# Decode attention with FFN on one core: a cut-up load ring that keeps twice as much V, with interleaved parts and warm-up matmuls

## The chip, the cores and the metric

The kernel runs on one core of a Trainium2 chip. The metric is the device time of one execution in microseconds. A verdict of faster or slower needs 2%.

In the profiles PE is TensorE running matmuls, PEld its weight loads, DVE VectorE, ACT ScalarE, POOL GpSimd, and SP the engine that issues the loads. PEclk, the granted clock, is the part of its full clock that TensorE was allowed. The DMA share is the time that the packets took, as a share of the time of 16 DMA engines; it can come out slightly above 1.

## The reference

Eight sequences (B = 8), one new token each, go twice through an attention block and an FFN block. Both attention blocks read the **same** K and V caches.

```python
# x: (8, 1, 640); k_cache, v_cache: (8, 32, 4096, 128); wq: (640, 4096); wo: (4096, 640)
def _A_ref(x, k_cache, v_cache, wq, wo):
    q = heads(x @ wq)                                        # 32 heads of 128
    p = softmax(einsum("bhqd,bhkd->bhqk", q, k_cache) * Dh ** -0.5)
    return flat(einsum("bhqk,bhkd->bhqd", p, v_cache)) @ wo
def _B_ref(x, w1, w2):
    return relu(x @ w1) @ w2                                  # 640 -> 1728 -> 640
x = x + A(layernorm(x)); x = x + B(layernorm(x))
x = x + A(layernorm(x)); x = x + B(layernorm(x))
```

K and V are 256 MiB each in bf16 and are used twice, so without reuse 1 GiB has to come from HBM. Layer 1 of a sequence needs all of its layer 0, so a K or V tile read for layer 0 can serve layer 1 only if it stays in SBUF for that long.

## The kernel before

The unit of work is a *visit*: one pair of heads of one sequence in one layer, 256 visits in all. A K or V tile of a visit is [128 partitions, 64 keys, 128], 2 MiB; each partition receives one contiguous run of 16 KiB. Visits of layer 0 of the next sequence stand between the two layers of a sequence, to give its FFN time.

```python
RING = 4
KEEP = ((0, 64), (1, 32))          # last head pair: 64 of 64 keys of V kept; the one before: 32
...
kv = ctx.enter_context(tc.tile_pool(name="kv", bufs=RING))
...
def load_k(i):
    K_tiles[i] = kv.tile([P, J, Dh], BF16, name="K_sb", tag="kv")
    nc.sync.dma_start(out=K_tiles[i], in_=pair_src(A_k_cache, b, hp))

def load_v(v):                      # (cut)
    if kk and layer == 0:           # stays in SBUF until layer 1
        kept[b, hp] = rpool.tile([P, kk, Dh], BF16, name=f"V_keep{hp}")
        nc.sync.dma_start(out=kept[b, hp], in_=src[:, :kk, :])
    if kk < J:
        V = kv.tile([P, J, Dh], BF16, name="V_sb", tag="kv")
        nc.sync.dma_start(out=V[:, kk:, :], in_=src[:, kk:, :])

def score(i):                       # q.k: multiply on DVE in place, sum over d on PE
    for w in PARTS:                 # 4 parts of 32 of the 128 d
        nc.vector.tensor_tensor(out=part, in0=part, in1=<q broadcast>, op=ALU.mult)
        for k in range(lo, lo + w, RW):
            nc.tensor.matmul(s_tiles[i], lhsT=ident, rhs=K[:, :, k : k + RW], ...)
```

In each loop pass the kernel scores visit i and attends visit i - 3, and loads K two visits ahead and V two visits ahead of its use.

Of the kernel before, what the change touches and what calls it, by code (L numbers as in the profile page):

```python
# [14 lines left out]
RING = 4  # L15
KEEP = ((0, 64), (1, 32))
PARTS = (32, 32, 32, 32)
# [13 lines left out]
def kernel(  # L31
# [12 lines left out]
    nc = tc.nc  # L44
# [22 lines left out]
    kv = ctx.enter_context(tc.tile_pool(name="kv", bufs=RING))  # L67
    rpool = ctx.enter_context(tc.tile_pool(name="rpool", bufs=1))
# [67 lines left out]
    def ln_steps(b0, nb, xln):  # L136
# [26 lines left out]
        def std():  # L163
            st["std"] = sm.tile([P, nb], FP32, name="std", bufs=1)
            nc.scalar.activation(out=st["std"], in_=st["var"], func=ACT.Sqrt, bias=eps_c, scale=1.0 / D)

# [10 lines left out]
    def ffn_steps(layer, b):  # L177
# [3 lines left out]
        cut1 = [f_i * FC // 3 for f_i in range(4)]  # L181
# [21 lines left out]
        def down(k):  # L203
            if k == 0:
                st["y_ps"] = ps.tile([P, DC], FP32, name="ch_ps")
            for c in range(k * DC // 3, (k + 1) * DC // 3):
# [11 lines left out]
        steps += [("P", lambda k=k: up(k)) for k in range(3)] + [("A", relu)]  # L218
        steps += [("P", lambda k=k: down(k)) for k in range(3)] + [("D", add)]
# [7 lines left out]
    FA = 3 * NP // 4  # L227
    FA -= FA % GP
    order0 = list(range(NP))

    NG = NP // GP
    order1 = [hp for g in range(NG - 1, -1, -1) for hp in [NP - NG + g] + list(range(g, NP - NG, NG))]
    order2 = [NP - 1, NP - 3, NP - 2, NP - 4] + order0[:-GP]
    visits = [(0, 0, hp, 1) for hp in order0]
    for b in range(B - 1):
        nxt = [(0, b + 1, hp, 1) for hp in order0]
        if b + 1 < B - 1:
            visits += nxt[:FA] + [(1, b, hp, NG) for hp in order1] + nxt[FA:]
        else:
            cur = [(1, b, hp, 1) for hp in order2]  # L240
            visits += nxt[:FA] + cur[:GP] + nxt[FA:] + cur[GP:]
    visits += [(1, B - 1, hp, NG) for hp in order1]
# [4 lines left out]
    keep = {NP - 1 - n: keys for n, keys in KEEP}  # L247
    last_of = {}
    for v, (layer, b, hp) in enumerate(visits):
        last_of[layer, b] = v  # L250

    K_tiles, V_tiles, kept, qb_tiles, s_tiles, S_tiles, invL_tiles, oT_tiles, oy_tiles, q_tiles = (
        {} for _ in range(10)
    )
    blk_ps = {}

# [3 lines left out]
    def load_k(i):  # L260
        layer, b, hp = visits[i]
        K_tiles[i] = kv.tile([P, J, Dh], BF16, name="K_sb", tag="kv")
        nc.sync.dma_start(out=K_tiles[i], in_=pair_src(A_k_cache, b, hp))

    def load_v(v):

        layer, b, hp = visits[v]
        kk = keep.get(hp, 0)
        src = pair_src(A_v_cache, b, hp)
        pieces = []  # L270
        if kk and layer == 0:
            kept[b, hp] = rpool.tile([P, kk, Dh], BF16, name=f"V_keep{hp}")
            nc.sync.dma_start(out=kept[b, hp], in_=src[:, :kk, :])
        if kk:
            pieces.append((0, kk, kept[b, hp]))
        if kk < J:
            V = kv.tile([P, J, Dh], BF16, name="V_sb", tag="kv")
            nc.sync.dma_start(out=V[:, kk:, :], in_=src[:, kk:, :])
            pieces.append((0, J, V))
        V_tiles[v] = pieces  # L280

    def project_q(i):
# [5 lines left out]
        assert sorted(group) == list(range(first, last, q_step[i]))  # L288
        xl = xlns[layer, b]
# [17 lines left out]
    def score(i):  # L307

        s_tiles[i] = ps.tile([P, J, RW], FP32, name="s_ps", bufs=2)
        K, q = K_tiles.pop(i), qb_tiles.pop(i)  # L310
        lo = 0
        for w in PARTS:
            part = K[:, :, lo : lo + w]
            nc.vector.tensor_tensor(out=part, in0=part, in1=_free(q[:, lo : lo + w], [(0, J), (1, w)]), op=ALU.mult)  # L314
            for k in range(lo, lo + w, RW):
                nc.tensor.matmul(  # L316
                    s_tiles[i], lhsT=ident, rhs=K[:, :, k : k + RW], start=(k == 0), stop=(k + RW == Dh)
                )
# [221 lines left out]
```

## Time and profile before

| | before |
|---|---|
| median time | 2537.75 us (four runs, 2537.68 to 2537.89) |
| moved by DMA | 1065.84 MB |
| PE / DVE busy | 74% / 60% |
| mean granted PE clock | 0.854 |

Slices, queues and chain of waits of the kernel before. In the first three lines each digit or number is one fortieth of the span; DMA digits are busy tenths of the 16 DMA engines, GB/s what they moved.

```profile
PEclk8878898888888889888888888888888888888887
DMA  9999999999999999999999999999999999999997
GB/s 394 415 412 426 427 425 427 426 425 422 423 427 424 427 421 420 427 425 425 427 418 428 425 426 426 417 427 426 426 426 420 426 426 425 410 426 426 427 425 309
DMA packets 83190, 1065.84 MB, mean 420 GB/s; under 512 B 8468, under 2 KB 14292, under 8 KB 17492
q1 hardware_dynamic: 83028, 1063.54, 99.4%
DMA 65%; PE 21%; DVE 14%; issue 0%; ACT 0%; SPq 0%; DVEq 0%; ACTq 0%
...
L314 DVE TENSOR_TENSOR K_sb<-K_sb,qb 128x2048 bf16<-128x2048 bf16 x1024 | 1185.7, 1221 | 422.7 <-DMA K_sb<-in_A_k_cache_dram 422.3
```

The load queue is busy 99.4% of the span, and DVE, which starts each visit, idles 422 us for K. The kernel is bound by DMA.

### The profile page before, as it was taken

The numbers are of one execution on the slowest core, as the hardware profiler recorded it, in microseconds if no ns is written. First come the engines' busy times: TensorE is split into PE (matmuls) and PEld (weight loads), VectorE is DVE, ScalarE is ACT, GpSimd is POOL, SyncE is SP. The second block draws the span as 40 slices with busy tenths as digits, with TensorE's granted clock in tenths as the row PEclk, the third lists the DMA queues.
The fourth block names the chain that finished last, engine by engine and source line by source line (L and its number), as shares of the span: only waits on it lengthen the run. The fifth ranks groups of instructions, "written<-read, shape, count | busy, mean of one in ns | idle before, by whom it ended". The sixth has DMA issues, their size and how long they took to land.

```text
span 2536.4 us, 36119 instructions
## 1 busy us (share of the span) xinstructions
PE 1877.8 (74%) x15270; PEld 870.8 (34%) x15270; DVE 1520.8 (60%) x2476; ACT 504.9 (20%) x1578; POOL 2.1 (0%) x15
## 2 busy tenths in 40 slices
PE   5657777787777877778777787777877777768776
PEld 2223333343333433334333343333433333333333
DVE  5445665666655656656566566656666566656664
ACT  1111211122112222112221122122211122212221
POOL 0000000000000000000000000000000000000000
PEclk8878898888888889888888888888888888888887
DMA  9999999999999999999999999999999999999997
GB/s 394 415 412 426 427 425 427 426 425 422 423 427 424 427 421 420 427 425 425 427 418 428 425 426 426 417 427 426 426 426 420 426 426 425 410 426 426 427 425 309
DMA packets 83190, 1065.84 MB, mean 420 GB/s; under 512 B 8468, under 2 KB 14292, under 8 KB 17492
## 3 DMA queue, kind: packets, MB, share of 16 engines
q1 hardware_dynamic: 83028, 1063.54, 99.4%
q8 instruction: 119, 1.95, 0.3%
q14 instruction: 43, 0.35, 0.0%
HBM read 1063.50 MB, written 0.01 MB: 419 GB/s over the span
## 4 chain that ended last, share of the span: by engine, by line
DMA 65%; PE 21%; DVE 14%; issue 0%; ACT 0%; SPq 0%; DVEq 0%; ACTq 0%
DMA K_sb<-in_A_k_cache_dram 64%; PE s_ps L316 19%; DVE K_sb L314 13%; PE o_ps L379 1%; DMA V_sb<-in_A_v_cache_dram 1%; PE ch_ps L209 0%; PE q_ps L294 0%; ACT o_sb L384 0%; PE blk_ps L361 0%; PE oy_ps L404 0%; PE ch_ps L189 0%; DVE hmx L337 0%; PE oy_ps L390 0%; DVE xT L411 0%; PE blk_ps L333 0%
## 5 line engine op out<-in xcount | busy, mean ns | idle before, releaser
L316 PE MATMUL s_ps<-K_sb,ident 128*128 128x512 bf16 x4096 | 1277.8, 467 | 557.6 <-DVE K_sb L314 524.7
L314 DVE TENSOR_TENSOR K_sb<-K_sb,qb 128x2048 bf16<-128x2048 bf16 x1024 | 1185.7, 1221 | 422.7 <-DMA K_sb<-in_A_k_cache_dram 422.3
L316 PEld LDWEIGHTS <-ident 128*128 128x128 bf16 x4096 | 468.7, 115 | 1267.8 <-issue 794.9
L384 ACT CAST o_sb<-o_ps 104x512 bf16<-104x512 f32 x256 | 150.0, 586 | 1723.0 <-PE blk_ps L333 1195.5
L379 PE MATMUL o_ps<-V_sb,P 128*8 128x512 bf16 x3712 | 250.8, 381 | 4.9 <-DMA V_sb<-in_A_v_cache_dram 4.9
L337 DVE TENSOR_REDUCE hmx<-blk_ps 2x2 f32<-2x128 f32 x128 | 35.6, 278 | 265.9 <-PE blk_ps L333 265.9
L354 ACT ACTIVATE P<-S_sb,nmax 64x64 bf16<-64x64 f32 x512 | 187.1, 365 | 8.5
L326 DVE TENSOR_REDUCE S_sb<-s_ps 128x64 f32<-128x512 f32 x256 | 175.4, 685 | 0.0
L379 PEld LDWEIGHTS <-P 128*8 128x8 bf16 x4096 | 99.2, 85 | 106.7 <-issue 59.3
L411 DVE TENSOR_TENSOR xT<-xT,oy_ps 128x5 f32<-128x5 f32 x256 | 38.6, 151 | 141.0 <-PE oy_ps L404 141.0
L404 PEld LDWEIGHTS <-wo_sb 128*128 128x128 bf16 x2560 | 80.9, 96 | 92.0 <-issue 92.0
L367 DVE RECIPROCAL invL<-blk_ps 128x4 f32<-128x4 f32 x128 | 23.4, 183 | 147.3 <-PE blk_ps L361 147.3
L404 PE MATMUL oy_ps<-oT,wo_sb 128*128 128x1 bf16 x2560 | 103.0, 165 | 0.2 <-DVE oT L397 0.2
L354 ACT ACTIVATION_READ_ACCUMULATOR P<-S_sb,nmax 64x1 f32 x512 | 94.5, 185 | 0.0
L390 PE MATMUL oy_ps<-dsel,o_sb 104*128 104x2 bf16 x1024 | 64.3, 166 | 36.6 <-ACT o_sb L384 36.6
L303 ACT CAST qb<-q_ps 128x512 bf16<-128x512 f32 x64 | 37.5, 586 | 245.7 <-DVE K_sb L314 240.8
L390 PEld LDWEIGHTS <-o_sb 104*128 104x128 bf16 x1024 | 44.5, 98 | 92.6 <-ACT o_sb L384 66.8
L361 PEld LDWEIGHTS blk_ps<-lrow,ones_c 128*128 128x128 f32 x256 | 48.7, 191 | 20.3 <-ACT P L354 1.9
L345 PE MATMUL blk_ps<-diag,onesb_c 2*128 2x4 bf16 x128 | 20.4, 159 | 33.2 <-DVE diag L341 31.5
L209 PE MATMUL ch_ps<-hT,w_sb 128*128 128x1 bf16 x1120 | 43.1, 165 | 2.0 <-ACT hT L200 0.3
L294 PE MATMUL q_ps<-wq_sb,xln 128*64 128x512 bf16 x320 | 41.7, 391 | 2.9 <-DMA wq_sb<-in_A_wq_dram 2.9
L209 PEld LDWEIGHTS <-w_sb 128*128 128x128 bf16 x1120 | 40.1, 96 | 9.4 <-PE oy_ps L404 5.5
(53 smaller groups left out, 503.8 us busy)
## 6 DMA issues: line engine op xcount, KB each, us to landing
K_sb<-in_A_k_cache_dram SPq DMA_DIRECT2D x256, 2048.0 KB, 13.0
V_sb<-in_A_v_cache_dram SPq DMA_DIRECT2D x224, 2048.0 KB, 16.9
V_sb<-in_A_v_cache_dram SPq DMA_DIRECT2D x16, 1024.0 KB, 17.7
V_keep<-in_A_v_cache_dram SPq DMA_DIRECT2D x8, 2048.0 KB, 17.6
V_keep<-in_A_v_cache_dram SPq DMA_DIRECT2D x8, 1024.0 KB
wq_sb<-in_A_wq_dram SPq DMA_DIRECT2D x4, 1280.0 KB, 19.7
wo_sb<-in_A_wo_dram SPq DMA_DIRECT2D x4, 1280.0 KB, 25.7
w_sb<-in_B_w_dram SPq DMA_DIRECT2D x1, 2160.0 KB, 28.6
```

Of the source, the lines that this page charges most:

```text
L209: nc.tensor.matmul(st["y_ps"][:, c : c + 1], lhsT=w2_sb[:fs, f, c * P : (c + 1) * P], rhs=st["hT"][:fs, f : f + 1], start=(f == 0), stop=( ...
L294: nc.tensor.matmul(q_ps[hh * HP : (hh + 1) * HP], lhsT=_free(xl[:, c : c + 1], [(0, HP)]), rhs=wv[:, c, first : last : q_step[i], hh, :], ...
L314: nc.vector.tensor_tensor(out=part, in0=part, in1=_free(q[:, lo : lo + w], [(0, J), (1, w)]), op=ALU.mult)
L316: nc.tensor.matmul(s_tiles[i], lhsT=ident, rhs=K[:, :, k : k + RW], start=(k == 0), stop=(k + RW == Dh))
L326: nc.vector.tensor_reduce(out=S_tiles[k][:, j, :], in_=s_tiles.pop(i), axis=AX.X, op=ALU.add)
L354: nc.scalar.activation(out=P2[k % 2][r, j, :, hh], in_=S[r, j, :], func=ACT.Exp, bias=nmax[r, j, hh : hh + 1], scale=inv_sqrt_dh, accum_ou ...
L361: nc.tensor.matmul(L_ps, lhsT=ones_f, rhs=lrow2[k % 2].rearrange("p j h -> p (j h)"), start=True, stop=True)
L379: nc.tensor.matmul(o_ps[32 * c : 32 * c + 8, :], lhsT=P2[k % 2][:, j, lo : lo + 4, :], rhs=V[:, lo : lo + 4, :], start=(g == 0), stop=(g = ...
L384: nc.scalar.copy(out=o_sb, in_=o_ps[:104, :])
L390: nc.tensor.matmul(oy_tiles[v][:, :2], lhsT=o_sb[:, i, :], rhs=dsel[:104, i, :], start=(i == 0), stop=(i == 3))
L404: nc.tensor.matmul(oy_tiles[v][:, 2 + c : 3 + c], lhsT=wo_sb[:, 2 * hp + hh, c * P : (c + 1) * P], rhs=oT[:, hh : hh + 1], start=(hh == 0) ...
L411: nc.vector.tensor_tensor(out=xT[:, b, :], in0=xT[:, b, :], in1=oy_tiles.pop(v)[:, 2:], op=ALU.add)
```

## The change: its intent, and the diff

Nearly the same SBUF is used otherwise. The ring of four tiles and the separate 1.5 kept tiles become one arena of 11 units of 1 MiB (half the keys of a tile). Loads take two adjacent units where at least four of the five pairs hold no kept half ("whole": 16 KiB per partition), otherwise one unit at a time ("half": 8 KiB per partition). Six halves of V are kept per sequence, 3 tiles for 1.5. Each unit is given back as soon as its half was used. The work of a visit is spread between the four parts of the score; WARM adds two matmuls that compute nothing before each of two of these parts.

```diff
-RING = 4
-KEEP = ((0, 64), (1, 32))
+UNITS = 11
+KEEP = ((0, 2), (1, 2), (2, 1), (3, 1))
+NCUT = 2
+WARM = 2
...
+        nc.scalar.activation(out=st["s1"][:, :1], in_=eps_c, func=ACT.Exp)   # after Sqrt
...
-    FA = 3 * NP // 4
+    FA = NP // 2
...
+    arena = kv.tile([P, UNITS * JH, Dh], BF16, name="arena")
...
+    def roomy():
+        k = kept_units()
+        return sum(1 for u in range(0, UNITS - 1, 2) if not {u, u + 1} & k) >= 4
...
+    def load_whole(which, v):                     # two adjacent units, one DMA
+    def load_half(which, v, h):                   # one unit, half the keys
+    def load_kept(v, h):                          # a half of V that stays for layer 1
...
+    warm_ps = ps.tile([P, 512], FP32, name="warm_ps")
+    def score(i, n):
+        if n % 2 == 0:
+            for _ in range(WARM):
+                nc.tensor.matmul(warm_ps, lhsT=ident, rhs=wq_sb[:, 0, :512], start=True, stop=True)
+        if ("K", i) in pairs:
+            K, j0, nj, lo, w = unit(take("K", i, 0), 2), 0, J, n * Dh // 4, Dh // 4
+        else:                                     # 2 parts of 64 of the d for each half of the keys
+            h = n // 2
+            K, j0, nj, lo, w = unit(take("K", i, h)), h * JH, JH, n % 2 * Dh // 2, Dh // 2
...
+            part(0)
+            ... softmax_sum, gather_o, one FFN piece
+            part(1)
+            ... reduce, max, 1/sum, scale; first half of V if loaded in halves
+            part(2)
+            ... max turned, output projection, one FFN piece
+            part(3)
+            ... rest of V, exp, one FFN piece
```

(Cuts are marked by dots; the order of the visits changes with FA.)

More of the change, by code (lines that the diff above doesn't have):

```diff
@@ L14 @@
 AX = mybir.AxisListType
-RING = 4
-KEEP = ((0, 64), (1, 32))
-PARTS = (32, 32, 32, 32)
+UNITS = 11
+KEEP = ((0, 2), (1, 2), (2, 1), (3, 1))
+NCUT = 2
+WARM = 2
 ENG = mybir.EngineType
@@ L66 @@
     wres = ctx.enter_context(tc.tile_pool(name="wres", bufs=1))
-    kv = ctx.enter_context(tc.tile_pool(name="kv", bufs=RING))
-    rpool = ctx.enter_context(tc.tile_pool(name="rpool", bufs=1))
+    kv = ctx.enter_context(tc.tile_pool(name="kv", bufs=1))
     sm = ctx.enter_context(tc.tile_pool(name="sm", bufs=2))
@@ L180, in ffn_steps @@
         steps = ln_steps(b, 1, xf)
-        cut1 = [f_i * FC // 3 for f_i in range(4)]
+        cut1 = [f_i * FC // NCUT for f_i in range(NCUT + 1)]
         def up(k):
@@ L205, in down @@
                 st["y_ps"] = ps.tile([P, DC], FP32, name="ch_ps")
-            for c in range(k * DC // 3, (k + 1) * DC // 3):
+            for c in range(k * DC // NCUT, (k + 1) * DC // NCUT):
                 for f in range(FC):
@@ L216, in add @@
             nc.vector.tensor_tensor(out=dst[:, b, :], in0=xT[:, b, :], in1=st["y_ps"], op=ALU.add)
-        steps += [("P", lambda k=k: up(k)) for k in range(3)] + [("A", relu)]
-        steps += [("P", lambda k=k: down(k)) for k in range(3)] + [("D", add)]
+        steps += [("P", lambda k=k: up(k)) for k in range(NCUT)] + [("A", relu)]
+        steps += [("P", lambda k=k: down(k)) for k in range(NCUT)] + [("D", add)]
         if layer == 0:
@@ L224, in ffn_steps @@
         return steps
-    FA = 3 * NP // 4
-    FA -= FA % GP
+    FA = NP // 2
     order0 = list(range(NP))
-    NG = NP // GP
-    order1 = [hp for g in range(NG - 1, -1, -1) for hp in [NP - NG + g] + list(range(g, NP - NG, NG))]
-    order2 = [NP - 1, NP - 3, NP - 2, NP - 4] + order0[:-GP]
-    visits = [(0, 0, hp, 1) for hp in order0]
+    top = NP - 2 * GP
+    order1, step1 = [], []
+    if top >= 0:
+        for a in (1, 0):
+            order1 += [NP - 2 + a, top + a, NP - 4 + a, top + 2 + a]
+    step1 = [2] * len(order1) + [1] * (NP - len(order1))
+    order1 += [hp for hp in order0 if hp not in order1]
+    first = [(0, 0, hp, 1) for hp in order0]
+    visits = first
     for b in range(B - 1):
         nxt = [(0, b + 1, hp, 1) for hp in order0]
+        cur = [(1, b, hp, st) for hp, st in zip(order1, step1)]
         if b + 1 < B - 1:
-            visits += nxt[:FA] + [(1, b, hp, NG) for hp in order1] + nxt[FA:]
+            visits = visits + nxt[:FA] + cur + nxt[FA:]
         else:
-            cur = [(1, b, hp, 1) for hp in order2]
-            visits += nxt[:FA] + cur[:GP] + nxt[FA:] + cur[GP:]
-    visits += [(1, B - 1, hp, NG) for hp in order1]
+            visits = visits + nxt[:FA] + cur[:FA] + nxt[FA:] + cur[FA:]
+    visits = visits + [(1, B - 1, hp, st) for hp, st in zip(order1, step1)]
     q_step = [v[3] for v in visits]
@@ L246 @@
     assert NV == 2 * B * NP and NV % 2 == 0
-    keep = {NP - 1 - n: keys for n, keys in KEEP}
+    n_keep = {NP - 1 - n: halves for n, halves in KEEP}
     last_of = {}
@@ L250 @@
         last_of[layer, b] = v
-    K_tiles, V_tiles, kept, qb_tiles, s_tiles, S_tiles, invL_tiles, oT_tiles, oy_tiles, q_tiles = (
-        {} for _ in range(10)
-    )
+    LAG = 3
+    JH = J // 2
+    arena = kv.tile([P, UNITS * JH, Dh], BF16, name="arena")
+    qb_tiles, s_tiles, S_tiles, invL_tiles, oT_tiles, oy_tiles, q_tiles = ({} for _ in range(7))
     blk_ps = {}
+    owner = [None] * UNITS
+    freed = list(range(-UNITS, 0))
+    clock = [0]
+    where = {}
+    pairs = set()
+    kept = {}
@@ L257, in pair_src, with buddy, unit, free @@
+    reserved = set()
+    def buddy(u):
+        return u ^ 1 if u ^ 1 < UNITS else None
+    def unit(u, n=1):
+        return arena[:, u * JH : (u + n) * JH, :]
     def pair_src(cache, b, hp):
         return cache[b, 2 * hp : 2 * hp + 2].rearrange("h (pp j) d -> (h pp) j d", pp=HP)
-    def load_k(i):
-        layer, b, hp = visits[i]
-        K_tiles[i] = kv.tile([P, J, Dh], BF16, name="K_sb", tag="kv")
-        nc.sync.dma_start(out=K_tiles[i], in_=pair_src(A_k_cache, b, hp))
-    def load_v(v):
-        layer, b, hp = visits[v]
-        kk = keep.get(hp, 0)
-        src = pair_src(A_v_cache, b, hp)
-        pieces = []
-        if kk and layer == 0:
-            kept[b, hp] = rpool.tile([P, kk, Dh], BF16, name=f"V_keep{hp}")
-            nc.sync.dma_start(out=kept[b, hp], in_=src[:, :kk, :])
-        if kk:
-            pieces.append((0, kk, kept[b, hp]))
-        if kk < J:
-            V = kv.tile([P, J, Dh], BF16, name="V_sb", tag="kv")
-            nc.sync.dma_start(out=V[:, kk:, :], in_=src[:, kk:, :])
-            pieces.append((0, J, V))
-        V_tiles[v] = pieces
+    def free(u):
+        clock[0] += 1
+        owner[u] = None
+        freed[u] = clock[0]
@@ new lines, in spare, with kept_units, dma @@
+    def spare():
+        us = [u for u in range(UNITS) if owner[u] is None and u not in reserved]
+        return min(us, key=lambda u: freed[u]) if us else None
+    def kept_units():
+        return set(kept.values())
+    def roomy():
+        k = kept_units()
+        return sum(1 for u in range(0, UNITS - 1, 2) if not {u, u + 1} & k) >= 4
+    def dma(u, n, cache, v, h):
+        layer, b, hp = visits[v]
+        nc.sync.dma_start(out=unit(u, n), in_=pair_src(cache, b, hp)[:, h * JH : (h + n) * JH, :])
@@ new lines, in load_whole @@
+    def load_whole(which, v):
+        us = [u for u in range(0, UNITS - 1, 2)
+              if owner[u] is None and owner[u + 1] is None and not {u, u + 1} & (reserved | kept_units())]
+        if not us:
+            return False
+        u = min(us, key=lambda u: max(freed[u], freed[u + 1]))
+        pairs.add((which, v))
+        for h in range(2):
+            owner[u + h] = where[which, v, h] = u + h
+        dma(u, 2, A_k_cache if which == "K" else A_v_cache, v, 0)
+        return True
@@ new lines, in load_half @@
+    def load_half(which, v, h):
+        u = spare()
+        if u is None:
+            return False
+        owner[u] = where[which, v, h] = u
+        dma(u, 1, A_k_cache if which == "K" else A_v_cache, v, h)
+        return True
+    def load_kept(v, h):
+        layer, b, hp = visits[v]
+        us = [u for u in reserved if owner[u] is None]
+        if not reserved:
+            us = [u for u in range(UNITS) if owner[u] is None and buddy(u) is not None]
+        if not us:
+            return False
+        u = min(us, key=lambda u: freed[u])
+        if u in reserved:
+            reserved.discard(u)
+        else:
+            reserved.add(buddy(u))
+        owner[u] = u
+        kept[b, hp, h] = where["V", v, h] = u
+        dma(u, 1, A_v_cache, v, h)
+        return True
@@ new lines, in v_halves @@
+    def v_halves(v):
+        layer, b, hp = visits[v]
+        n = n_keep.get(hp, 0)
+        out = []
+        for h in range(2):
+            if h >= 2 - n:
+                out.append((h, "keep" if layer == 0 else "kept"))
+            else:
+                out.append((h, "half"))
+        return out
+    late = {}
+    NG = NP // GP
+    for g in range(NG):
+        if g:
+            late.setdefault(max(0, GP * (g - 1)), []).append(lambda g=g: load_wq(g))
+        late.setdefault(GP * g + (0 if g == 0 else 1), []).append(lambda g=g: load_wo(g))
@@ new lines, with expand @@
+    late.setdefault(NP - 7 if NP > 8 else 0, []).append(load_w1)
+    late.setdefault(NP - 5 if NP > 8 else 0, []).append(load_w2)
+    todo = []
+    seen = [0]
+    def expand():
+        i = seen[0]
+        v = i - LAG
+        seen[0] += 1
+        if i >= 2:
+            todo.extend((lambda f=f: f() or True) for f in late.get(i - 2, []))
+        vh = v_halves(v) if 0 <= v < NV else []
+        whole = roomy()
+        vs = []
+        if whole and [how for _, how in vh] == ["half", "half"]:
+            vs = [[lambda: load_whole("V", v)]]
+        else:
+            for h, how in vh:
+                if how == "keep":
+                    vs.append([lambda h=h: load_kept(v, h)])
+                elif how == "half":
+                    vs.append([lambda h=h: load_half("V", v, h)])
+        ks = []
+        if i < NV:
+            if whole:
+                ks = [lambda: load_whole("K", i)]
+            else:
+                ks = [lambda h=h: load_half("K", i, h) for h in range(2)]
+        for n in range(2):
+            if n < len(ks):
+                todo.append(ks[n])
+            if n < len(vs):
+                todo.extend(vs[n])
@@ new lines, in feed, with take, done @@
+    def feed():
+        while todo or seen[0] < NV + LAG:
+            if not todo:
+                expand()
+                continue
+            if not todo[0]():
+                break
+            todo.pop(0)
+    def take(which, v, h):
+        if which == "V" and ("V", v, h) not in where:
+            layer, b, hp = visits[v]
+            where["V", v, h] = kept[b, hp, h]
+        return where[which, v, h]
+    def done(which, v, h):
+        layer, b, hp = visits[v]
+        u = where.pop((which, v, h))
+        if which == "V" and (b, hp, h) in kept:
+            if layer == 0:
+                return
+            del kept[b, hp, h]
+            if buddy(u) in reserved:
+                reserved.discard(buddy(u))
+        free(u)
@@ L282, in project_q, with xln_ready @@
+    def xln_ready(i):
+        layer, b, hp = visits[i]
+        return (layer, b) in xlns and not (layer == 1 and chain)
     def project_q(i):
@@ L288, in project_q @@
         assert sorted(group) == list(range(first, last, q_step[i]))
+        assert xln_ready(i)
         xl = xlns[layer, b]
@@ L305, in take_q, with release @@
             qb_tiles[k] = qb[:, (visits[k][2] - first) // q_step[i], :]
-    def score(i):
-        s_tiles[i] = ps.tile([P, J, RW], FP32, name="s_ps", bufs=2)
-        K, q = K_tiles.pop(i), qb_tiles.pop(i)
-        lo = 0
-        for w in PARTS:
-            part = K[:, :, lo : lo + w]
-            nc.vector.tensor_tensor(out=part, in0=part, in1=_free(q[:, lo : lo + w], [(0, J), (1, w)]), op=ALU.mult)
-            for k in range(lo, lo + w, RW):
-                nc.tensor.matmul(
-                    s_tiles[i], lhsT=ident, rhs=K[:, :, k : k + RW], start=(k == 0), stop=(k + RW == Dh)
-                )
-            lo += w
-        assert lo == Dh
+    warm_ps = ps.tile([P, 512], FP32, name="warm_ps")
[3 more added lines that the diff above has]
+                nc.tensor.matmul(warm_ps, lhsT=ident, rhs=wq_sb[:, 0, :512], start=True, stop=True)
+        if n == 0:
+            s_tiles[i] = ps.tile([P, J, RW], FP32, name="s_ps", bufs=2)
+        q = qb_tiles[i]
+        if ("K", i) in pairs:
+            K, j0, nj, lo, w = unit(take("K", i, 0), 2), 0, J, n * Dh // 4, Dh // 4
+            over = (0, 1) if n == 3 else ()
+        else:
+            h = n // 2
+            K, j0, nj, lo, w = unit(take("K", i, h)), h * JH, JH, n % 2 * Dh // 2, Dh // 2
+            over = (h,) if n % 2 else ()
+        part = K[:, :, lo : lo + w]
+        nc.vector.tensor_tensor(out=part, in0=part, in1=_free(q[:, lo : lo + w], [(0, nj), (1, w)]), op=ALU.mult)
+        for k in range(lo, lo + w, RW):
+            nc.tensor.matmul(
+                s_tiles[i][:, j0 : j0 + nj, :], lhsT=ident, rhs=K[:, :, k : k + RW], start=(k == 0), stop=(k + RW == Dh)
+            )
+        return over
+    def release(which, v, halves):
+        for h in halves:
+            done(which, v, h)
+        if halves:
+            feed()
     def reduce_s(i):
@@ L326, in reduce_s, with softmax_max, softmax_turn, softmax_diag @@
         nc.vector.tensor_reduce(out=S_tiles[k][:, j, :], in_=s_tiles.pop(i), axis=AX.X, op=ALU.add)
-    def softmax_a(k):
+    def softmax_max(k):
         mrow = sm.tile([P, 2], BF16, name="mrow")
         nc.vector.tensor_reduce(out=mrow, in_=S_tiles[k], axis=AX.X, op=ALU.max)
+        return mrow
+    def softmax_turn(k, mrow):
         blk_ps[k] = ps.tile([P, P + 8], FP32, name="blk_ps")
         nc.tensor.matmul(blk_ps[k][:2, :P], lhsT=mrow, rhs=ident, start=True, stop=True)
-    def softmax_b(k):
+    def softmax_diag(k):
         hmx = sm.tile([2, 2], FP32, name="hmx")
@@ L343, in softmax_b, with softmax_exp @@
         )
+        return diag
+    def softmax_exp(k, diag):
         gmax = blk_ps[k][:, P : P + 4]
@@ L357, in softmax_b, with softmax_sum @@
                 )
-    def softmax_c(k):
+    def softmax_sum(k):
         L_ps = blk_ps[k][:, P + 4 : P + 8]
@@ L363, in softmax_c, with softmax_inv @@
         )
-    def softmax_d(k):
+    def softmax_inv(k):
         invL_tiles[k] = sm.tile([P, 2, 2], FP32, name="invL")
@@ L369, in softmax_d, with attend, copy_o @@
         )
-    def attend(v):
+    def attend(v, h):
         k, j = divmod(v, 2)
-        pieces = V_tiles.pop(v)
-        n = J // 4
-        for t in range(n):
-            c, g = divmod(t, n // 4)
-            lo = 4 * (4 * g + c)
-            V = next(V for k0, nk, V in pieces if k0 <= lo < k0 + nk)
-            nc.tensor.matmul(
-                o_ps[32 * c : 32 * c + 8, :], lhsT=P2[k % 2][:, j, lo : lo + 4, :], rhs=V[:, lo : lo + 4, :],
-                start=(g == 0), stop=(g == n // 4 - 1), tile_position=(0, 32 * c),
-            )
+        V = unit(take("V", v, h))
+        n = J // 16
+        for c in range(4):
+            for g in range(h * n // 2, (h + 1) * n // 2):
+                lo = 4 * (4 * g + c)
+                nc.tensor.matmul(
+                    o_ps[32 * c : 32 * c + 8, :], lhsT=P2[k % 2][:, j, lo : lo + 4, :],
+                    rhs=V[:, lo - h * JH : lo - h * JH + 4, :],
+                    start=(g == 0), stop=(g == n - 1), tile_position=(0, 32 * c),
+                )
+        done("V", v, h)
+        feed()
+    def copy_o():
         o_sb = sm.tile([104, 4, Dh], BF16, name="o_sb", bufs=1)
@@ L411, in add_y, with chain_d, chain_p @@
         nc.vector.tensor_tensor(out=xT[:, b, :], in0=xT[:, b, :], in1=oy_tiles.pop(v)[:, 2:], op=ALU.add)
-    late = {}
-    for g in range(NG):
-        if g:
-            late.setdefault(max(0, GP * (g - 1)), []).append(lambda g=g: load_wq(g))
-        late.setdefault(GP * g + (0 if g == 0 else 1), []).append(lambda g=g: load_wo(g))
-    late.setdefault(NP - 7 if NP > 8 else 0, []).append(load_w1)
-    late.setdefault(NP - 5 if NP > 8 else 0, []).append(load_w2)
-    def load_first(i, v):
-        if RING == 4 and i + 2 < NV:
-            load_k(i + 2)
-        if RING == 3 and 0 <= v + 1 < NV:
-            load_v(v + 1)
-    def load_second(i, v):
-        if RING == 4 and 0 <= v + 2 < NV:
-            load_v(v + 2)
-        if RING == 3 and i + 2 < NV:
-            load_k(i + 2)
+        if last_of[layer, b] == v:
+            chain.extend(ffn_steps(layer, b))
     chain = []
-    def slot(early=True):
-        while early and chain and chain[0][0] == "D":
+    def chain_d():
+        while chain and chain[0][0] == "D":
             chain.pop(0)[1]()
-        if chain and chain[0][0] != "D":
+    def chain_p():
+        if chain and chain[0][0] == "P":
             chain.pop(0)[1]()
-    LAG = 3
+        if chain and chain[0][0] == "A":
+            chain.pop(0)[1]()
     with tc.manual_schedule(engines={ENG.PE, ENG.DVE, ENG.Activation, ENG.SP}):
         load_wq(0)
-        load_k(0)
-        load_k(1)
+        feed()
         xT_ps = ps.tile([P, B * DC], FP32, name="ch_ps")
@@ L458, with part @@
         take_q(0)
-        for i in range(NV + LAG):
-            v = i - LAG
-            new = i < NV
-            blk = i // 2 - 1 if i % 2 == 0 and i >= 2 and i // 2 - 1 < NV // 2 else None
-            if new:
-                score(i)
-                for f in late.get(i, []):
-                    f()
+        o_sb = None
+        for i in range(NV + LAG + 1):
+            v, w = i - LAG, i - LAG - 1
+            new, att, fin = i < NV, 0 <= v < NV, 0 <= w
+            k_new = i // 2 - 1 if i % 2 == 0 and 2 <= i <= NV else None
+            k_sum = v // 2 if att and v % 2 == 0 else None
+            def part(n):
+                over = score(i, n) if new else ()
+                release("K", i, over)
+            part(0)
+            if k_sum is not None:
+                softmax_sum(k_sum)
+            if fin:
+                gather_o(w, o_sb)
+            chain_p()
+            part(1)
+            if 1 <= i <= NV:
+                reduce_s(i - 1)
+            mrow = softmax_max(k_new) if k_new is not None else None
+            if k_sum is not None:
+                softmax_inv(k_sum)
+            if fin:
+                scale_o(w)
+            chain_d()
+            split = att and ("V", v) not in pairs
+            if split:
+                attend(v, 0)
+            part(2)
+            if mrow is not None:
+                softmax_turn(k_new, mrow)
+            if fin:
+                project_o(w)
+            chain_p()
+            if i + 1 < NV and (i + 1) % GP == 0 and i + 1 not in q_tiles:
+                project_q(i + 1)
+            part(3)
@@ L468 @@
             if i + 1 in q_tiles:
                 take_q(i + 1)
-            load_first(i, v)
-            if v >= 0 and v % 2 == 0:
-                softmax_c(v // 2)
-            if v >= 0:
-                o_sb = attend(v)
-            load_second(i, v)
-            if 1 <= i <= NV:
-                reduce_s(i - 1)
-            if blk is not None:
-                softmax_a(blk)
-            if v >= 0 and v % 2 == 0:
-                softmax_d(v // 2)
-            if v - 1 >= 0:
-                scale_o(v - 1)
-                project_o(v - 1)
@@ L485 @@
-            slot()
-            if blk is not None:
-                softmax_b(blk)
-            if v - 1 >= 0:
-                add_y(v - 1)
-                if last_of[visits[v - 1][:2]] == v - 1:
-                    chain += ffn_steps(*visits[v - 1][:2])
-            slot()
-            slot(early=False)
-            if i + 2 < NV and (i + 2) % GP == 0:
-                project_q(i + 2)
-            if v >= 0:
-                gather_o(v, o_sb)
-        scale_o(NV - 1)
-        project_o(NV - 1)
@@ L501 @@
-        add_y(NV - 1)
-        chain += ffn_steps(*visits[NV - 1][:2])
+            diag = softmax_diag(k_new) if k_new is not None else None
+            if fin:
+                add_y(w)
+            chain_d()
+            if att:
+                if not split:
+                    attend(v, 0)
+                attend(v, 1)
+            if diag is not None:
+                softmax_exp(k_new, diag)
+            if att:
+                o_sb = copy_o()
+            chain_p()
+            if i + 2 < NV and (i + 2) % GP == 0 and xln_ready(i + 2):
+                project_q(i + 2)
@@ L503 @@
+        assert not todo and seen[0] == NV + LAG
         for _, step in chain:
```

## The prediction

> **What bounds it now.** DMA. The slices view shows DMA nine tenths or more busy in 39 of 40 slices; the queue table gives q1 99.4% of 16 engines' span; the chain of waits is 65% DMA. PE (74%) and DVE (60%) have room: DVE waits 422 us for K loads. Where DMA share is 1.0 the rate is 424-428 GB/s; over 200-2500 us it averages 424.1. [...] Idle is small: a tail of 16 us (2520-2537, share 0.01), about 4 us at the start, single dips (318 GB/s in 2210-2220).
>
> **What the change does.**
> 1. Bytes. Before keeps 1.5 V tiles of 2 MiB per batch from layer 0 to layer 1; after keeps six halves (head pairs 15, 14 whole; 13, 12 half), 3 tiles. Saved: 8 x 3 MiB = 25.2 MB of 1065.8 MB; at 424.1 GB/s -59 us, all on the critical path while DMA is the bound.
> 2. Buffers. Same SBUF: ring of 4 plus 1.5 kept tiles before, 11 units of 1 MiB after. With nothing kept, 10 units in pairs: deeper than before. With six kept, 5 units instead of 8 MiB, for an estimated 15 of each 32 visits. Estimate: a half takes 2.46 us at 426 GB/s, a small load (x_bf) 1.6 us to landing, so a unit must be released within 5x2.46-2.46-1.6 = 8.2 us of landing. A K half needs two DVE parts (2x1.16) and PE's tail, some 4 us: enough on an undisturbed visit, not always where a q projection or the FFN chain, which falls in this mode, holds PE. I allow 3-12 us.
> 3. Compute. Added: 1024 warm-up matmuls of 128x512, 0.21-0.43 us each, 0.9-1.7 us per visit; K halves use 32 matmuls of 256 columns for 16 of 512 (estimate: under 1 us); an Exp after each Sqrt, moving the 1.28 us table load. Parts are interleaved with softmax and output work. DVE stays near 6.1 us per visit, PE 7-8, against 9.5 of DMA: off the critical path. [...] the trace shows ident weight loads every 0.43 us at 0.5, 0.21 at full. I expect a mean granted clock above 0.90 (0.854 before).
> 4. First uses in layer 1: about 8.0 us of DMA per visit over eight visits, close to PE's need; freed kept units let loads run ahead, so no loss.
> 5. Start and tail: unchanged within 2 us.
>
> **Time.** 2537.75 - 59 + 2 (smaller loads) + 3 to 12 (starved moments), less up to 8 (dips gone with the deeper ring) = about 2481 us. Range 2464 to 2508. Faster by over 2% (below 2487) 0.62, within 2% 0.36, slower 0.02.
>
> **What would show it.** Right: 1040.7 MB; share 1.0 and 422-427 GB/s in steady slices; chain of waits mostly DMA; half loads in about half of the visits; tail 16 us. Wrong: step 2, if five-unit stretches show share below 0.97 and the DMA queue waiting on PE; step 3, if PE is over 90% busy and the chain turns to PE or DVE; step 1, if bytes fall less.
>
> **What would make it wrong.** Coarse waits between units of the one arena; pairs fragmented when whole loads return; slower half loads; compute pacing the five-unit stretches. Each gives 2490-2530. Queues removing every dip would give 2465.

2537.75 - 59 + 2 + 3 to 12, less up to 8, came to about 2481 us. That the rate can't rise, and that the added matmuls would lift the clock above 0.90, are expectations without a shown ground.

## More of the kernel before

Note the packets too: a packet of K or V is one contiguous run of one partition (83,028 less the 17,492 under 8 KB are 65,536, which is 128 for each of 512 loads). The next lines are stretches of the kernel before, with columns: stretch, length, PE, PEld, DVE, ACT and POOL busy (instructions), granted clock, DMA share, GB/s.

```profile
120.00:200.00 80.00, 45.74 (x316) 19.97 (x314) 35.58 (x57) 10.46 (x35) 0.00 (x0) 0.76 1.02 413
200.00:500.00 300.00, 223.34 (x1742) 101.16 (x1742) 183.20 (x293) 59.40 (x192) 0.00 (x0) 0.87 1.01 426
```

The first stretch has weight loads in runs of 1280 and 3456 bytes among the K and V loads; its rate is 413 GB/s at a share of 1.02, not 426. So a full share doesn't mean a full rate.

## The result, and the profile after

| | before | after |
|---|---|---|
| median time | 2537.78 us (12 runs) | 2506.48 us (8 runs, 2505.54 to 2508.2) |
| moved by DMA | 1065.84 MB | 1041.16 MB |
| PE / DVE busy | 74% / 60% | 79% / 61% |
| mean granted PE clock | 0.854 | 0.921 |

The ratio is 0.9877 with a 95% interval of 0.9867 to 0.9887: 1.2% faster. Ratios here are the mean time of one kernel's runs over that of the other's of the same rounds, so not quite the ratio of the medians quoted.

The same lines of the kernel after:

```profile
PEclk8888999989989999899998999888998899988997
DMA  9999999999999999999999999999999999999997
GB/s 393 414 414 414 412 421 425 425 412 417 422 427 424 413 419 423 426 421 410 415 424 426 422 412 418 425 426 421 400 419 425 427 420 409 419 425 414 415 421 306
DMA packets 118933, 1041.16 MB, mean 416 GB/s; under 512 B 12436, under 2 KB 18260, under 8 KB 21460
q1 hardware_dynamic: 118740, 1038.39, 99.6%
DMA 67%; PE 24%; DVE 6%; SPq 2%; issue 1%; ACT 0%; DVEq 0%; ACTq 0%
...
L470 DVE TENSOR_TENSOR arena<-arena,qb 128x2048 bf16<-128x2048 bf16 x1024 | 1207.5, 1221 | 778.7 <-DMA arena<-in_A_k_cache_dram 772.7
...
arena<-in_A_v_cache_dram SPq DMA_DIRECT2D x272, 1024.0 KB, 10.0
arena<-in_A_k_cache_dram SPq DMA_DIRECT2D x272, 1024.0 KB, 11.3
arena<-in_A_k_cache_dram SPq DMA_DIRECT2D x120, 2048.0 KB, 21.1
arena<-in_A_v_cache_dram SPq DMA_DIRECT2D x96, 2048.0 KB, 18.0
```

The bytes are those predicted, the queue is as busy as before, the chain still lies on DMA, and DVE now idles 773 us for K. DMA is even more clearly the bound. But the rate in the steady slices moves between 427 and about 400, where it lay mostly near 426. There are 35,700 more packets for fewer bytes, and 544 half loads, in 53% of the K visits. Stretches of the kernel after, columns as above: the first two with whole loads, the third with halves, the last two where the FFN of a sequence falls in the time of halves.

```profile
1600.00:1650.00 50.00, 38.63 (x269) 15.56 (x269) 29.30 (x46) 7.36 (x24) 0.00 (x0) 0.86 1.01 427
1930.00:1960.00 30.00, 25.57 (x168) 9.96 (x167) 17.94 (x29) 5.03 (x19) 0.00 (x0) 0.80 1.01 427
1800.00:1850.00 50.00, 38.03 (x392) 22.59 (x390) 32.77 (x51) 9.87 (x34) 0.00 (x0) 1.00 1.01 419
1770.00:1780.00 10.00, 8.76 (x109) 6.10 (x110) 5.77 (x9) 1.50 (x7) 0.00 (x0) 0.66 0.95 378
1780.00:1790.00 10.00, 10.00 (x140) 6.80 (x136) 6.83 (x15) 0.59 (x1) 0.00 (x0) 1.00 0.96 376
```

In the third line the share is 1.01 as in the first two, and the rate is 419, not 427. In that stretch DMA isn't idle; it moves less while it is busy. In the last two lines the share falls as well, to 0.95: there something else is missing. From 1750 to 1790 us the load queue waited 17.5 us for PE and 16.0 us for DVE to give units back. Two losses, then, and the experiments have to size them:

- **Theory A, run length.** Each contiguous run costs a DMA engine a fixed time. Halves have runs of 8 KiB, so twice as many for the same bytes.
- **Theory B1, count of DMAs.** The cost is per DMA issued: 248 more of them.
- **The ring theory.** Five units of 1 MiB are too few, and DMA waits for units to come free.
- **Theory C, compute.** The added PE work holds units too long.

### The profile page after: what moved, and what is told of

Same layout as the page of the kernel before. It is cut to its first block, busy times and chain, and to the rows that moved or that the text cites. A ratio compares the mean times of both kernels' runs of the same rounds, so it can differ in the third digit from the quotient of the medians. Undisturbed runs are those within 1.5% of the kernel's fastest.

```text
span 2505.7 us, 43199 instructions
## 1 busy us (share of the span) xinstructions
PE 1972.8 (79%) x18470; PEld 1026.6 (41%) x18470; DVE 1528.3 (61%) x2476; ACT 512.4 (20%) x1604; POOL 2.0 (0%) x15
## 2 busy tenths in 40 slices
DMA packets 118933, 1041.16 MB, mean 416 GB/s; under 512 B 12436, under 2 KB 18260, under 8 KB 21460
## 3 DMA queue, kind: packets, MB, share of 16 engines
q1 hardware_dynamic: 118740, 1038.39, 99.6%
## 4 chain that ended last, share of the span: by engine, by line
DMA 67%; PE 24%; DVE 6%; SPq 2%; issue 1%; ACT 0%; DVEq 0%; ACTq 0%
DMA arena<-in_A_k_cache_dram 66%; PE s_ps L472 15%; DVE arena L470 6%; PE o_ps L545 4%; PE warm_ps L457 1%; DMA arena<-in_A_v_cache_dram 1%; PE ch_ps L210 1%; PE oy_ps L575 1%; SPq L98 1%; PE q_ps L438 1%; PE ch_ps L190 0%; SPq L84 0%; PE oy_ps L561 0%; PE blk_ps L497 0%; PE blk_ps L528 0%
## 5 line engine op out<-in xcount | busy, mean ns | idle before, releaser
L470 DVE TENSOR_TENSOR arena<-arena,qb 128x2048 bf16<-128x2048 bf16 x1024 | 1207.5, 1221 | 778.7 <-DMA arena<-in_A_k_cache_dram 772.7
L472 PE MATMUL s_ps<-arena,ident 128*128 128x256 bf16 (+1 forms) x6272 | 1173.0, 328 | 509.7 <-DVE arena L470 507.8
L472 PEld LDWEIGHTS <-ident 128*128 128x128 bf16 x6272 | 599.7, 101 | 918.9 <-issue 376.4
L457 PE MATMUL warm_ps<-wq_sb,ident 128*128 128x512 bf16 x1024 | 330.3, 406 | 0.0
L545 PE MATMUL o_ps<-arena,P 128*8 128x512 bf16 x4096 | 309.6, 392 | 2.5 <-DMA arena<-in_A_v_cache_dram 2.4
L514 ACT ACTIVATE nmax<-blk_ps 128x4 f32<-128x4 f32 x128 | 22.1, 173 | 1019.0 <-PE blk_ps L512 1019.0
L457 PEld LDWEIGHTS <-ident 128*128 128x128 bf16 x1024 | 73.2, 104 | 181.0 <-issue 168.4
L545 PEld LDWEIGHTS <-P 128*8 128x8 bf16 x4096 | 66.9, 84 | 149.1 <-issue 128.5
L575 PEld LDWEIGHTS <-wo_sb 128*128 128x128 bf16 x2560 | 91.8, 96 | 27.0 <-issue 2.8
L561 PEld LDWEIGHTS <-o_sb 104*128 104x128 bf16 x1024 | 67.9, 112 | 32.7 <-issue 17.4
L501 DVE TENSOR_REDUCE hmx<-blk_ps 2x2 f32<-2x128 f32 x128 | 35.6, 278 | 61.0 <-PE blk_ps L497 50.3
L568 DVE TENSOR_TENSOR oT<-oy_ps,invL 128x2 bf16<-128x2 f32 x256 | 37.1, 145 | 21.3 <-PE oy_ps L561 20.4
## 6 DMA issues: line engine op xcount, KB each, us to landing
wo_sb<-in_A_wo_dram SPq DMA_DIRECT2D x4, 1280.0 KB, 25.7
```

Source lines behind the costliest of these rows:

```text
L457: nc.tensor.matmul(warm_ps, lhsT=ident, rhs=wq_sb[:, 0, :512], start=True, stop=True)
L470: nc.vector.tensor_tensor(out=part, in0=part, in1=_free(q[:, lo : lo + w], [(0, nj), (1, w)]), op=ALU.mult)
L472: nc.tensor.matmul(s_tiles[i][:, j0 : j0 + nj, :], lhsT=ident, rhs=K[:, :, k : k + RW], start=(k == 0), stop=(k + RW == Dh))
L545: nc.tensor.matmul(o_ps[32 * c : 32 * c + 8, :], lhsT=P2[k % 2][:, j, lo : lo + 4, :], rhs=V[:, lo - h * JH : lo - h * JH + 4, :], start=( ...
L561: nc.tensor.matmul(oy_tiles[v][:, :2], lhsT=o_sb[:, i, :], rhs=dsel[:104, i, :], start=(i == 0), stop=(i == 3))
L575: nc.tensor.matmul(oy_tiles[v][:, 2 + c : 3 + c], lhsT=wo_sb[:, 2 * hp + hh, c * P : (c + 1) * P], rhs=oT[:, hh : hh + 1], start=(hh == 0) ...
```

## The experiments

Twelve runs; all passed the comparison with the reference. (So did the three with chunks misplaced on purpose: the comparison isn't fine enough to notice, and nothing is concluded from its passing.)

### Run length and count of DMAs by themselves, in the kernel before

The ring, the order and the compute of the kernel before stay. Only the source of a tile is cut: partition p gets NS chunks that lie apart, so one DMA of 2 MiB has runs of 8 KiB (NS = 2) or 4 KiB (NS = 4); `ndma` = 2 splits it into two DMAs.

```diff
-        return cache[b, 2 * hp : 2 * hp + 2].rearrange("h (pp j) d -> (h pp) j d", pp=HP)
+        return cache[b, 2 * hp : 2 * hp + 2].rearrange("h s d -> (h s) d").rearrange("(n p j) d -> p n j d", n=NS, p=P)
...
-        nc.sync.dma_start(out=K_tiles[i], in_=pair_src(A_k_cache, b, hp))
+        load(K_tiles[i], pair_src(A_k_cache, b, hp), 0, J)      # ndma DMAs; V alike
```

One DMA, runs of 8 KiB:

> Kernel before, each K and V load still one DMA of 2 MiB, but in runs of 8 KiB instead of 16 KiB (every partition gets two chunks that lie 1 MiB apart; wrong result on purpose, same work). Theory A (each contiguous run costs each DMA engine a fixed time, estimate 11.7 ns, worked out from 427 GB/s in 16 KiB stretches against 419 GB/s in 8 KiB stretches of the changed kernel): 3904 runs more per engine, +46 us, about 2583 us. Theory B (the cost is per DMA, or it is the five-unit ring, or compute): same count of DMAs and same ring, so 2538 us within 4.

Two DMAs, runs of 8 KiB:

> As b_run8k, but the two runs of each partition come by two DMAs of 1 MiB. Theory A: the runs are the same, so within 5 us of b_run8k, about 2583 us. Theory B1 (cost per DMA, about 0.1 us each if the 248 additional DMAs of the changed kernel explain its missing 25 us): 488 DMAs more, +49 us on top of whatever b_run8k shows. Ring theory: 2538 us.

One DMA, runs of 4 KiB:

> As b_run8k, with four runs of 4 KiB per partition (wrong result on purpose). Theory A is linear in the number of runs: three times 46 us, about 2675 us, 404 GB/s in steady stretches. Theory B: 2538 us. If the cost isn't linear in runs (a threshold below 8 KiB), it shows as a time far from 2675.

| | time | against before (2537.84 us) | ratio (95%) |
|---|---|---|---|
| 8 KiB runs, one DMA | 2576.64 us | +38.8 us | 1.0152 (1.0137 to 1.0167) |
| 8 KiB runs, two DMAs | 2578.85 us | +41.0 us | 1.0161 (1.0146 to 1.0176) |
| 4 KiB runs, one DMA | 2644.35 us | +106.5 us | 1.0419 (1.0402 to 1.0436) |

The rate line and packet counts, first of the 8 KiB run with one DMA:

```profile
GB/s 389 410 408 419 420 419 418 420 419 418 414 419 419 419 417 413 420 420 418 420 413 420 419 419 420 409 420 420 418 420 414 419 420 418 412 419 420 418 415 305
q1 hardware_dynamic: 145492, 1063.54, 100.0%
```

and of the 4 KiB run:

```profile
GB/s 380 402 398 408 409 407 409 409 408 408 402 409 409 408 409 399 409 409 408 409 398 409 409 408 409 404 409 409 408 407 402 409 409 408 401 409 409 406 409 295
q1 hardware_dynamic: 273492, 1063.54, 101.1%
```

Bytes, count of DMAs, ring and compute are those of before, and the steady rate is 419 to 420 with 8 KiB, 408 to 409 with 4 KiB, for 426 with 16 KiB. The share stays at 100% and above. This shows theory A. The size: 62,464 packets more over 16 engines are 3,904 per engine, 38.8 us / 3,904 = 9.9 ns each; for 4 KiB 190,464 / 16 = 11,904 per engine and 106.5 us give 8.9 ns. My 11.7 ns was somewhat too high for this kernel and both expectations were missed on the high side, by 6 and 31 us; the cost of a run is not quite the same for 8 and 4 KiB. That the chunks lie elsewhere in HBM is no rival: the halves of the kernel after lie differently again and run at the same 419 GB/s. Splitting each load into two DMAs adds 2.2 us for 488 of them, some 5 ns each, where theory B1 wanted 100 ns: B1 falls.

### Run length and ring depth by themselves, in the kernel after

Nothing is kept, so that all 512 tiles are loaded. First all whole, then all in halves with the deep ring, then all in halves with the ring that the kernel after has while six halves are kept.

```diff
-KEEP = ((0, 2), (1, 2), (2, 1), (3, 1))
+KEEP = ()                          # all three
-        return sum(1 for u in range(0, UNITS - 1, 2) if not {u, u + 1} & k) >= 4
+        return False                # the second and third
-UNITS = 11
+UNITS = 5                          # the third
```

> The changed kernel with nothing kept, so every load is a whole one of 2 MiB with 16 KiB runs, and the ring is ten units in pairs. 25.2 MB more than before are moved: at 424.1 GB/s 2538 + 59 = 2597 us if the new schedule and deeper ring gain nothing; down to 2587 if they remove the dips. It is the base for the next two runs.

> As d_whole, but every load is two halves of 1 MiB with 8 KiB runs, ring of 11 units. Theory A: 4096 runs more per engine at 11.7 ns, 48 us over d_whole, about 2645 us. Ring theory: the ring is deep, so equal to d_whole within 5 us.

> As d_half11 with a ring of only five units all the time. Theory A with a small ring part (I count some 6 us of more low-rate stretches in the changed kernel, over about half of its visits): 8 to 16 us over d_half11, about 2657 us. Ring theory (the five-unit stretches cost all of the missing 28 us): about 50 us over d_half11.

| | time | ratio to before (95%) |
|---|---|---|
| all whole, ten units | 2597.01 us | 1.0234 (1.0219 to 1.0249) |
| all halves, 11 units | 2645.42 us | 1.0425 (1.0407 to 1.0442) |
| all halves, five units | 2652.42 us (2646.64 to 2655.66) | 1.0450 (1.0434 to 1.0465) |

The steady part (200 to 2400 us) of the three, columns as above:

```profile
200.00:2400.00 2200.00, 1693.59 (x13926) 751.50 (x14159) 1315.24 (x2145) 442.79 (x1388) 0.00 (x0) 0.90 1.01 425
200.00:2400.00 2200.00, 1640.54 (x17031) 994.37 (x17260) 1307.73 (x2095) 431.86 (x1359) 0.00 (x0) 0.95 1.01 418
200.00:2400.00 2200.00, 1642.07 (x17031) 996.15 (x17259) 1307.59 (x2094) 431.77 (x1359) 0.00 (x0) 0.95 1.01 416
```

Three things follow.

The first run moves 25.2 MB more than before and takes 59.4 us more than the 2537.62 us of its rounds: 424 GB/s. The price of bytes in the prediction was right, and the new schedule with its deeper ring gains nothing by itself in this test.

The second has the same schedule and a deep ring, and takes 48.4 us more: 48.4 us / 1024 half loads = 47 ns per half load. It gives the price of halves, including the matmuls of 256 columns and the second DMA, in this very kernel. Per run and engine that is 48.4 us / 4096 = 11.8 ns, for 9.9 in the kernel before; the difference is not explained.

The third adds 7.0 us, a bit less than my 8 to 16, for *all* visits in a ring of five, though its four runs spread over 9 us. The 50 us that the ring theory asked for aren't there. Expecting the ring to be a small part held.

### The warm-up matmuls taken away

```diff
-WARM = 2
+WARM = 0
```

> The changed kernel without its 1024 warm-up matmuls. Theory A and the ring theory (DMA is the bound throughout): within 6 us of 2506, with PE busy lower and the granted clock falling from 0.92 towards 0.87. Theory C (the added PE work holds units too long in the five-unit stretches): faster, 2490-2500. If the warm clock is what keeps the five-unit stretches fed, slower, 2515 or more.

Measured: 2515.38 us (2510.95 to 2516.69), ratio 0.9908 (0.9893 to 0.9923), which doesn't overlap the 0.9867 to 0.9887 of the kernel after. The granted clock fell to 0.863. It is slower by 9 us, though PE has 1024 matmuls less and DMA makes the same loads (1038.39 MB in the load queue of the kernel after). Theory C falls, and so does my reading that PE is wholly off the critical path. A stretch of this run in the FFN, and then the same place in the sequence of another:

```profile
860.00:870.00 10.00, 10.00 (x163) 7.14 (x164) 5.85 (x9) 0.82 (x3) 0.00 (x0) 0.75 0.88 326
1470.00:1480.00 10.00, 10.00 (x134) 6.62 (x134) 4.71 (x7) 2.90 (x13) 0.00 (x0) 0.53 0.85 310
```

PE is busy for the whole stretch, at a clock of 0.75 and 0.53; the DMA share is 0.88 and 0.85. In the kernel after the lowest 10 us of the steady part have 376 GB/s, here 310. As I read it, PE at a low clock gives units back late, just where a small ring, an FFN and half loads meet. That the 9 us come from the clock alone is argued from these stretches; no run changed the clock and nothing else.

### Fewer half loads by an earlier return to whole loads

```diff
-        return sum(1 for u in range(0, UNITS - 1, 2) if not {u, u + 1} & k) >= 4
+        return sum(1 for u in range(0, UNITS - 1, 2) if not {u, u + 1} & k) >= 3
```

> The changed kernel with whole loads already where three pairs hold no kept half (four before), so that fewer visits load halves. Theory A: about a third of the half loads go; 5 to 9 us faster than 2506, about 2499 us, unless the ring of three pairs starves. Ring theory: three pairs of 2 MiB are as shallow as five halves or worse, so 2506 or slower.

Measured: 2511.49 us (2510.0 to 2516.97), ratio 0.9901 (0.9886 to 0.9916). The interval just touches that of the kernel after (0.9867 to 0.9887). Theory A alone was wrong here: the half loads fell from 544 to 400, worth 144 x 0.047 = 6.8 us, and the time rose by 5. Of 228 stretches of 10 us in the steady part 26 were under 410 GB/s, against 22 of the kernel after, and in 6 the DMA share was under 0.97, against 2. As I read it, not tested by itself, three pairs of 2 MiB are a shallower ring than five halves: a pair comes back only when all of it was used. What the runs saved was lost to waiting; the sum below puts that at 14 us.

### Fewer half loads by what is kept and when it is used

The six halves come from three whole head pairs instead of four, so the ring is whole again two visits sooner; then, layer 1 also uses its second kept tile at once.

```diff
-KEEP = ((0, 2), (1, 2), (2, 1), (3, 1))
+KEEP = ((0, 2), (1, 2), (2, 2))                                                    # both
-            order1 += [NP - 2 + a, top + a, NP - 4 + a, top + 2 + a]
+            order1 += [NP - 2 + a, NP - 4 + a, top + a, top + 2 + a]               # the second
```

> The changed kernel with the same six kept halves taken from three whole head pairs (15, 14, 13) and not from four, so that the ring is whole again two visits earlier: 464 half loads instead of 544, bytes as before the edit. Theory A with the measured 47 ns per half load (48.4 us over 1024 halves) says 80 x 0.047 = 4 us faster than the changed kernel: about 2502 us. Ring theory: also a little faster, since the five-unit time is shorter.

> As v_keep6, and layer 1 uses its kept tiles at its visits 1, 2 and 5 and not 1, 3 and 5: 432 half loads. Theory A: another 1.5 us, about 2500 us. If two visits in a row without a V load leave DMA waiting for compute, 2503 or more.

Measured: 2502.16 us (2501.96 to 2506.54), ratio 0.9864 (0.9849 to 0.9878), and 2500.79 us (2500.55 to 2506.27), ratio 0.9859 (0.9845 to 0.9874). Both medians fall within 1 us of what the price per half load said. The intervals overlap that of the kernel after (0.9867 to 0.9887), and one run of four in each lies some 5 us above the others, so the gain of 4 to 6 us agrees with the count but isn't proven by the intervals alone. The second is the fastest kernel found.

### A seventh half kept

```diff
+KEEP = ((0, 2), (1, 2), (2, 2), (3, 1))
...
+        if n_keep[hp] == 1:                        # this half goes to the single unit
+            us = [UNITS - 1] if owner[UNITS - 1] is None else []
```

> v_keep6 and a seventh half kept (half of head pair 12, in the single unit), so the ring falls to four units: 8.4 MB less, 488 half loads. With the rate theory alone 2597.0 - 58.7 MB at 424.1 GB/s + 488 x 0.047 = 2482 us. If the ring of four starves (a unit must then be released within 4 x 2.46 - 2.46 - 1.6 = 5.8 us of landing, an estimate as in the prediction), 2490 to 2510.

With the four kept head pairs used in the first four visits of layer 1 (`order1 = [NP - 1, NP - 2, NP - 3, NP - 4]` and then the rest, in steps of 1):

> v_keep7, with layer 1 using its four kept head pairs in its first four visits: 440 half loads, 2479 us by the rate theory alone. The four visits need only nine half loads for sixteen, so compute may be the bound there for some us per batch: then above v_keep7.

Measured: 2628.6 us (2622.66 to 2635.86), ratio 1.0359 (1.034 to 1.0379), and 2631.74 us (2616.11 to 2639.89), ratio 1.0381 (1.0352 to 1.0409). Both are far outside what I wrote, even for starving. Lines of the first:

```profile
GB/s 395 415 368 378 382 423 426 389 397 382 425 426 384 378 371 425 427 367 369 379 426 427 372 372 401 427 426 356 366 403 426 426 363 367 404 392 367 364 417 315
q1 hardware_dynamic: 114132, 1030.00, 96.0%
...
1400.00:1430.00 30.00, 24.78 (x173) 9.92 (x171) 18.45 (x30) 5.60 (x21) 0.00 (x0) 0.85 1.01 426
1460.00:1470.00 10.00, 8.36 (x74) 3.49 (x73) 6.02 (x11) 2.51 (x10) 0.00 (x0) 1.00 0.52 206
1500.00:1510.00 10.00, 6.99 (x69) 3.65 (x68) 5.11 (x10) 2.51 (x10) 0.00 (x0) 1.00 0.85 329
...
1444.09 25.17 SPq L301 DMA_DIRECT2D arena<-in_A_v_cache_dram  x2
```

Here DMA really is idle: the queue's share is 96.0%, the rate lies between 356 and 389 GB/s in most slices with a small ring and at 426 to 427 in those with whole loads. Near 1460 us almost half of a stretch is lost; on the load queue a 25 us pause stands there (the last line: the first of its two DMAs was issued at 1444.1 us, the second at 1468.9). The order of the 728 loads, worked out from the kernel's code and matched with the queue, names the load after the pause: it is the seventh half. The edit lets it go only to the single unit, which the other half of the same tile had just taken, and all later loads stood behind it while the kernel's order had given back eight of the 11 units. The kernel's order has the same block in each of the eight sequences; its length is quoted here for one. An estimate: eight times the 4.8 us lost at a share of 0.52 are some 40 of the 147 us of the sum below, a fault of this edit and not of the number of units. How much of the rest is the ring of four was not separated; no run has four units and nothing kept.

### The sum

"By rate" is 2597.0 us (all whole, nothing kept), less the kept bytes at 424.1 GB/s, plus 47 ns per half load. What is left is time that neither bytes nor runs explain.

| kernel | kept MB | half loads | by rate | measured | left |
|---|---|---|---|---|---|
| after | 50.3 | 544 | 2478.3 + 25.7 = 2504.0 | 2506.5 | 2.5 |
| six halves of three pairs | 50.3 | 464 | 2478.3 + 21.9 = 2500.2 | 2502.2 | 2.0 |
| the same, used sooner | 50.3 | 432 | 2478.3 + 20.4 = 2498.7 | 2500.8 | 2.1 |
| no warm-up | 50.3 | 544 | 2504.0 | 2515.4 | 11.4 |
| whole from three pairs on | 50.3 | 400 | 2478.3 + 18.9 = 2497.2 | 2511.5 | 14.3 |
| seven halves | 58.7 | 488 | 2458.5 + 23.1 = 2481.6 | 2628.6 | 147.0 |

For the kernel after only 2.5 us are left for starving, about as much as its eight runs spread. Nearly all of the gain that was missed is the price of its half loads.

## Why the prediction was right or wrong

The time, 2506.5 us, lies inside the range (2464 to 2508), at its far end; the centre of 2481 was 25 us too low, and the case given the best chance, faster by over 2%, didn't come about. That the time fell inside the range is partly luck: the prediction's own list of what would make it wrong has "slower half loads" with 2490 to 2530, and that is what happened.

- **The bound: right.** DMA before, and DMA after by every view.
- **Step 1, bytes: right.** 1041.2 MB for the predicted 1040.7, and the price of 59 us for 25.2 MB was measured on the way up, 59.4 us.
- **The term "+ 2 (smaller loads)": the step that failed.** Measured by 1024 half loads it is 47 ns each, so 25.7 us for the 544 of the kernel after, thirteen times what I put down. The mechanism was on my list ("slower half loads"), but I gave it 2 us without costing it. The prediction also held that only bytes or DMA idle time can be taken away because the rate can't rise. This left out that the rate can fall at full share, here to 419 GB/s at 1.01: of the signs that the prediction named, 422 to 427 GB/s in steady slices was missed, with slices down to 400. The stretch with 413 GB/s at a share of 1.02 in the trace before could have warned of it.
- **Step 2, the ring of five: right in kind, too large in size.** I allowed 3 to 12 us; the sum leaves 2.5. The estimate that a unit may be held 8.2 us is not contradicted: five units in all visits cost 7 us over the whole kernel. The stretches at share 0.95 are this loss; only 2 of the 228 are under the 0.97 that I had named as the sign of failure.
- **Step 3, compute off the critical path: half right.** PE stayed at 79% and the clock rose above 0.90 as predicted. But the warm-ups aren't neutral: without them 9 us are lost. What lowers the clock was not shown. Measured is its mean, 0.863 without warm-ups for 0.921 with them, and the profile's busy time doesn't tell where it falls: from 1470 us of the run without them PE counts as busy for all 10 us, at a clock of 0.53.
- **Step 4, first uses: no loss seen.** The second order, with two kept tiles used in a row, leaves 2.1 us, no more than the others.
- **Step 5, start and tail: right.** From the landing of the last K or V load to the end it takes 15.3 us, before and after (from 2521.1 to 2536.4 us and from 2490.4 to 2505.7 us).
- **"Less up to 8 (dips gone)": wrong.** The all-whole run shows no gain of that kind. Its dips did go: no stretch of 10 us in the steady part is under a share of 0.97, for three in the kernel before. But the steady rate is 425 GB/s for 424.

## What to carry to other kernels

Read a DMA-bound stretch by two numbers, its share and its rate: a full share with a lower rate (here 1.01 and 419 GB/s) meant that the loads had got less efficient, and longer runs helped (48.4 us between all halves and all whole), not more buffers (7.0 us between five units and 11); a falling share (here 0.95 to 0.96) went with loads that waited for buffers (17.5 us for PE and 16.0 us for DVE in 40 us). When a tile is cut to free buffers sooner, price the additional runs first, here 47 ns per half of 1 MiB over 128 partitions, against the bytes that it saves, here 2.5 us per half kept and sequence; the trade was good, but it brought only 31 of the 59 us that the bytes alone promised. And test one buffer less before believing in a margin: five units cost little, and the kernel that kept one half more lost more than the whole gain. There, look at the order first: where loads are issued in order, one that may go to a single place stops every load behind it (here for 25 us).
